# Attention followed by two expert layers: the sums of exponentials as matrix products with ones, four groups side by side, and GpSimd left with one kind of element-wise work

## The chip, the cores and the metric

The kernel runs on one core of one Trainium2 chip. The number that counts is the device time in microseconds (us) of one execution of the whole program; the runs of the kernel before have a median of 1322.9 us. Engine names in the rows: PE is TensorE (PEld its weight loads), DVE is VectorE, ACT is ScalarE, POOL is GpSimd, SP is SyncE, whose queue issues nearly all DMAs.

## The reference

Three stages, all in fp32. The change is in the first.

```
def _attn_ref(q, k, v, g_q, g_k):              # q, k, v: (4, 12, 448, 64)
    q_n, k_n = (rmsnorm(q, g_q), rmsnorm(k, g_k))
    scale = 1.0 / np.sqrt(q.shape[-1])
    scores = scale * np.matmul(q_n, k_n.transpose(0, 1, 3, 2))
    scores = scores - np.max(scores, axis=-1, keepdims=True)
    attn = np.exp(scores)
    attn = attn / (np.sum(attn, axis=-1, keepdims=True) + 1e-09)
    return np.matmul(attn, v).astype(np.float32)
...
    x = np.ascontiguousarray(attn_out.transpose(0, 2, 1, 3)).reshape(B * S, H * D)
    x = _moe_ref(x=x, **moe_kwargs)       # logits = x @ w_gate, 8 experts of 224 tokens, relu
    return _moe2_ref(x=x, **moe2_kwargs)  # h = x @ w_in; (h * cos(h)) @ w_out
```

## The kernel before

Two plans run one after the other. The first holds the attention, the router's logits, and, between them, the turning of 56 of 96 pieces of the last layer's 64-bit weights into pairs of 32-bit ones (tiles `nr` and `na`). The second holds the router, the experts, the last layer and the other 40 pieces.

**How work gets its place.** Every operation is first recorded as a `Step` with an engine, a cost in microseconds (`Plan.cost`) and what it reads and writes. `Plan.run` then places the steps in a simulated time and issues them in that order. `Plan.either` records one operation with two ways, VectorE and GpSimd; the planner takes the one that by its costs ends first. With `plan.shared` false, `either` means VectorE alone. On the chip each engine works through its instructions in the order that came out, and waits where an operand isn't there.

**The attention.** 48 heads are worked through as 24 pairs of two heads. For a pair, `front` loads queries and keys and gets the norms' roots (`squares`, `norm`); `turn` scales queries and keys by them (tile `qn`, by `either`), transposes them on TensorE (bank `t`) and splits them into a high and a low part (`hl` for queries, `kh` and `kl` for keys); SyncE's DMAs copy the parts into `tk` and `qs`. `shifts` gets upper bounds of the scores (seven products into bank `s`, seven maxima on VectorE into `cm`), and `copy` brings them as row `cr` into `qs`. `scores` multiplies (bank `st`, two of them), and ScalarE takes the exponential into a tile `pf`, 448 queries wide, with 112 keys in its partitions; four such tiles make one head. `weigh` multiplies the `pf` tiles with the values into bank `po`, the two heads of a pair side by side in 64 columns of the array each. `rows` gets the denominators and the router's logits, `tail` transposes and scales the output (`xk`), and `pair` stores it.

**What the change touches.** In `scores`, the four `pf` tiles of a head are added to one tile `sm` by three additions, on VectorE or GpSimd as the planner likes: 144 in all, of which the order has 130 on GpSimd and 14 on VectorE. In `rows`, once for three pairs, `ones` multiplies the `sm` tiles of the three pairs side by side, 32 columns of the array each, in two steps (head 0, head 1); a third step of the same shape multiplies the outputs `xe` with the router's weights `wg`. All three go into bank `dn`. One copy on ScalarE and four transposes then bring sums and logits to where VectorE takes the reciprocal. The last three pairs are done one at a time, with the three products side by side. `EASY` sends the low part of the queries from pair 2 on to GpSimd (ScalarE makes a second copy `f` for it, since GpSimd's operand has to lie in SBUF). `zset` fills constants before the first pair, `mix` (`mx`) gets two 64x64 corners of the queries for a pair's fourth bound, and in `Narrow.plan` a clamp of `na` and the last subtraction (`nr`) go to VectorE or GpSimd. The helper's line is L47, so rows are told apart by tiles.

Of the kernel before, what the change touches and what calls it, by code (L numbers as in the profile page):

```python
# [50 lines left out]
class Plan:  # L51
# [4 lines left out]
    def __init__(self, nc):  # L56
        self.nc, self.steps, self.seen, self.group, self.rush = nc, [], {}, None, 0.0
        self.shared, self.ahead = True, 0.0
# [217 lines left out]
UP = 3  # L276
# [3 lines left out]
NPF = 10  # L280
NSM = 9
# [6 lines left out]
EASY = 2  # L288
# [18 lines left out]
def attention(tc, P, R, ident, q, k, v, g_q, g_k, w_gate, x_dram, L, other):  # L307
# [4 lines left out]
    with ExitStack() as ctx:  # L312
# [32 lines left out]
        dns = ring("dn", 1, [96, S])  # L345
        xks = ring("xk", 2, [CP, NC, 2 * UP * D])
        recs = ring("r", 2, [CP, NC, 3, 2])
# [6 lines left out]
        def zset(t, val):  # L354
            P.either("memset", t.bitcast(F32), val)
# [48 lines left out]
        for _ in range(NSM):  # L404
            zset(sms()[96:CP + 1], 1.0)
        for t in mix:
            zset(t, 0.0)
        ve.tensor_scalar(gcol[:, 2:3], gcol[:, 0:1], gcol[:, 1:2], None, op0=ALU.mult)
# [19 lines left out]
        def turn(P_, i, rs, j):  # L428

            if True:  # L430
# [3 lines left out]
                mul = P.vector.tensor_tensor if P_ == 0 and i and QND else partial(P.either, "tensor_tensor")  # L434
# [123 lines left out]
        def weigh(P_):  # L558

            po = bo()[:, :S]  # L560
            t = vals.pop(P_).rearrange("p h (c d) -> p h c d", d=D)
            for c in range(NC):
                def both():
                    for h in range(2):
                        pe.matmul(po[h * D:(h + 1) * D], t[:, h, c], exps.pop((P_, h, c)), start=c == 0, stop=c == NC - 1)

                block(both)
            outs[P_] = xes()
            sc.activation(outs[P_], po, AF.Copy)

        def rows(ps):


            pd, dn, r, n = bd(), dns(), recs(), len(ps)
            steps = [[(ones[:, h], sums_of.pop((y, h))) for y in ps] for h in range(2)]
            steps.append([(wg[:, y % NP], outs[y]) for y in ps])
            if n == 1:
                steps = [[(ones[:, 0], x[0][1]) for x in steps[0:2]] + steps[2]]
            for k, row in enumerate(steps):
                def some():  # L580
                    for g, (w, x) in enumerate(row):
                        pe.matmul(pd[32 * g:32 * g + 32, :S], w, x, start=k == 0, stop=k == len(steps) - 1)

                block(some)
            sc.activation(dn, pd[0:96, :S], AF.Copy)
            p = bt()[0:CP, 0:NC * 96].rearrange("p (c g x) -> p c g x", c=NC, g=3)
# [787 lines left out]
```

## Time and profile before

| | us |
|---|---|
| median of three runs (1319.28 to 1332.39) | 1322.9 |
| the profiled execution | 1326.97 |
| its span from the first to the last instruction | 1325.1 |
| attention, by the engines' work | 0 to about 440 |
| router's first round, until the first expert's rows arrive | about 440 to 470 |
| experts and last layer | 470 to 1320 |

The profiled execution is 4 us above the median. The profile gives each engine's busy time in a stretch, the clock that TensorE was granted (1.00 is 2.4 GHz; the other level, 1.2 GHz, is 0.50), and, for the idle time before an instruction, who ended it. A matmul of fp32 operands leaves two records, a transpose and a product of reduced-precision operands (`F32R`) one.

### The profile page before, as it was taken

The page shows a single profiled execution, that of the slowest core. Times are in us where ns is not written, and L with a number is a line of the kernel's source. Part 1 is how long each engine was busy: PE and PEld are TensorE (multiplying, and loading weights), DVE is VectorE, ACT ScalarE, POOL GpSimd, SP SyncE. Part 2 cuts the span into 40 slices and gives each one's busy share as a digit, 9 for nine tenths or more (in the row PEclk, how much of TensorE's full clock was granted, in tenths as well). Part 3 has the DMA queues.
Part 4 walks back from the last instruction along what each step waited for, and adds up shares of the span by engine and source line. Part 5 has one row for each costly group of instructions (what it writes and reads, how often), then busy time and mean ns, then how long its engine had stood idle before and what let it go on. Part 6 is the DMA issues. An engine that isn't in the chain of part 4 may idle for free.

```text
span 1325.1 us, 20895 instructions
## 1 busy us (share of the span) xinstructions
PE 1194.0 (90%) x6807; PEld 954.3 (72%) x6807; DVE 978.0 (74%) x2641; ACT 671.5 (51%) x1657; POOL 317.7 (24%) x349
## 2 busy tenths in 40 slices
PE   6888887888988489999988999999999999899996
PEld 4444443433433289988877998889998889899996
DVE  8879999999898987989858658918657917655601
ACT  5566665655445354667345437625437615444500
POOL 4667676656755100000000200000200000100001
PEclk9789998878678678999988899999899999899998
DMA  8768787877755256988885767794677793676762
GB/s 198 169 166 206 205 210 201 233 191 199 202 164 161 95 152 202 287 306 278 302 258 188 208 202 231 231 296 120 190 210 228 245 282 109 167 214 220 239 218 74
DMA packets 207951, 273.53 MB, mean 206 GB/s; under 512 B 17473, under 2 KB 178530, under 8 KB 201698
## 3 DMA queue, kind: packets, MB, share of 16 engines
q1 hardware_dynamic: 205282, 261.18, 67.4%
q0 software_dynamic: 2560, 11.01, 2.8%
q8 instruction: 54, 0.88, 0.3%
q14 instruction: 55, 0.45, 0.1%
HBM read 202.79 MB, written 36.46 MB: 181 GB/s over the span
## 4 chain that ended last, share of the span: by engine, by line
PE 46%; DMA 11%; DVE 9%; issue 2%; ACT 1%; POOL 1%; SPq 0%; POOLq 0%; DVEq 0%; ACTq 0%
PE acc L47 42%; DMA wx<-w_out 2%; DMA xr<-x,idx 2%; DMA w_out<-nr 2%; PE tr L47 1%; PE rt L47 1%; DMA ws<-in_moe_w_dram 1%; DMA nr<-in_moe_w_out_dram 1%; DMA AB<-rows 1%; DVE wx L47 1%; DVE na L47 1%; DVE AB L47 1%; DVE oh L47 1%; DMA wx<-w_in 1%; DVE r L47 1%
## 5 line engine op out<-in xcount | busy, mean ns | idle before, releaser
L47 PE MATMUL acc<-gh,wx 128*128 128x224 f32 (+1 forms) x1952 | 376.9, 320 | 4.5 <-DMA wx<-w_out 3.0
L47 PEld LDWEIGHTS acc<-gh,wx 128*128 128x128 f32 x1952 | 290.8, 198 | 20.9 <-DMA wx<-w_out 6.5
L47 PE MATMUL acc<-x2h,wx 128*128 128x448 f32 x768 | 226.3, 372 | 0.0
L1155 POOL DMA_INDIRECT xr<-x,idx x16 | 18.0, 1125 | 640.5 <-issue 211.2
L47 PEld LDWEIGHTS acc<-x2h,wx 128*128 128x128 f32 x768 | 146.3, 190 | 16.5 <-issue 5.0
L47 DVE TENSOR_TENSOR wx<-ws,wx 128x768 fp32r<-128x768 f32 (+1 forms) x112 | 119.8, 1071 | 47.2 <-ACT wx L1194 43.1
L1194 ACT ACTIVATE wx<-ws 128x768 fp32r<-128x768 f32 (+1 forms) x104 | 98.1, 943 | 98.4 <-PE acc L47 82.7
L47 PE MATMUL acc<-gl,wx 128*128 128x448 f32 (+1 forms) x400 | 146.3, 366 | 0.0
L47 PE MATMUL acc<-xe,wx 128*128 128x224 f32 x1152 | 141.5, 284 | 0.3 <-DVE wx L47 0.2
L47 PE MATMUL acc<-x2l,wx 128*128 128x448 f32 x384 | 141.5, 369 | 0.0
L47 PEld LDWEIGHTS acc<-xe,wx 128*128 128x128 f32 x1152 | 138.2, 200 | 1.6 <-ACT wx L1194 0.8
L47 ACT ACTIVATE pf<-st 112x448 f32<-112x448 f32 x192 | 98.4, 541 | 67.5 <-PE st L47 63.5
L47 PE MATMUL st<-qs,tk 128*112 128x448 f32 (+1 forms) x384 | 124.4, 440 | 5.8 <-ACT pf L47 5.2
L47 DVE TENSOR_REDUCE cm<-s 128x1 f32<-128x448 f32 (+1 forms) x169 | 100.0, 615 | 29.6 <-PE s L47 29.3
L47 ACT ACTIVATE oh<-oh 128x896 bf16<-128x896 bf16 x80 | 75.3, 942 | 78.8 <-DVE oh L47 78.5
L47 PE MATMUL po<-pf,vr 112*64 112x448 f32 x384 | 108.6, 653 | 0.2 <-ACT pf L47 0.2
L47 POOL TENSOR_TENSOR sm<-sm,pf 112x448 f32<-112x448 f32 x87 | 103.4, 1205 | 16.3 <-ACT pf L47 9.4
L47 PEld LDWEIGHTS st<-qs,tk 128*112 128x112 f32 (+1 forms) x384 | 72.5, 208 | 47.9 <-ACT pf L47 17.0
L47 PE MATMUL s<-tk,qs 128*128 128x448 f32 (+2 forms) x146 | 64.5, 481 | 40.0 <-DVE cm L47 30.1
L47 DVE SCALAR_TENSOR_TENSOR na<-nr,na 128x256 int32<-128x256 int32 x192 | 97.9, 529 | 1.2
L47 ACT ACTIVATE r<-r 128x448 f32<-128x448 f32 x128 | 73.2, 574 | 32.4 <-DVE r L47 30.7
L47 DVE TENSOR_SCALAR oh<-AB,b 128x896 bf16<-128x896 f32 x80 | 51.2, 683 | 50.7 <-DMA AB<-rows 45.1
(248 smaller groups left out, 1919.0 us busy)
## 6 DMA issues: line engine op xcount, KB each, us to landing
wx<-w_in SPq DMA_DIRECT2D x64, 768.0 KB
wx<-w_out SPq DMA_DIRECT2D x48, 1024.0 KB
ws<-in_moe_w_dram SPq DMA_DIRECT2D x64, 384.0 KB
ws<-in_moe_w_dram SPq DMA_DIRECT2D x48, 512.0 KB
nr<-in_moe_w_in_dram SPq DMA_DIRECT2D x48, 256.0 KB
w_in<-nr SPq DMA_DIRECT2D x48, 256.0 KB
nr<-in_moe_w_out_dram SPq DMA_DIRECT2D x48, 256.0 KB
w_out<-nr SPq DMA_DIRECT2D x48, 256.0 KB
```

The costliest lines, as they stand in the source:

```text
L47: self.plan.add([(self.eng, self.plan.cost(self.eng, name, out, r, kw), lambda: f(*args, **kw))], r, w)
L1155: P.add([("POOL", 1.03, lambda x=x, h=h: nc.gpsimd.indirect_dma_start(out=x, out_offset=None, in_=x_rows, in_offset=bass.IndirectOffsetOnA ...
L1194: P.add([("ACT", 0.093 + n * 0.1067, lambda: nc.scalar.activation(hi, s, AF.Copy)), ("DVE", 0.07 + n * 0.0667, lambda: nc.vector.tensor_co ...
```

## The change

The additions go, and so do the tiles `sm`. In `weigh`, after the value products of a pair, `ones` multiplies the `pf` tiles themselves: the four tiles of a head at once, each in 32 columns of the array of its own, head 0 and then head 1, into the four 32-partition groups of bank `dn`. The 17 extra partitions that bring the 1e-9 move from `sm` to `pf`. `rows` works for one pair at a time: one product of 32 columns for the logits, added into the first group, a copy of 128 partitions, and, in place of four transposes, four fp32 products with `pick`, a 128x32 matrix that adds the four groups while it transposes. So reciprocal, copy and store come once a pair and not once in three. There are 18 `pf` tiles for 10.

`P.shared = False` is set once constants are filled, so that `either` means VectorE for the clamps and subtractions of `Narrow`, for `mix` and for the router's count. `EASY` and the copy `f` go: the low part of all queries is VectorE's. Constants are filled by GpSimd alone. The scaling of queries and keys is VectorE's in the first three pairs and GpSimd's in all others. The planner's costs for TensorE change too (`Plan.cost`), for both plans, so that the order changes all over.

```diff
-            return max(out.free_size() / 2400.0 + 0.0015, 0.105 if rhs.dtype == F32R else 0.0467) * passes
+            if name == "matmul" and rhs.dtype == F32 and self.beside:
+                passes *= {32: 0.32, 64: 0.6}.get(out.partition_size(), 1)
+            return max(out.free_size() / 2333.0 + 0.011, 0.107 if rhs.dtype == F32R else 0.0467) * passes
...
-        pfs = ring("pf", NPF, [CP, S])
-        pfs2 = ring("f2", 1, [128, S])
-        sms = ring("sm", NSM, [CP + 1, S])
+        pfs = ring("pf", NPF, [CP + 1, S])
...
-                mul = P.vector.tensor_tensor if P_ == 0 and i and QND else partial(P.either, "tensor_tensor")
+                mul = P.vector.tensor_tensor if P_ < UP else P.gpsimd.tensor_tensor
...
-                    if P_ >= EASY:
-                        f = pfs2()
-                        sc.activation(f, p[:, :S], AF.Copy)
-                        P.gpsimd.tensor_tensor(lo, f, hi.bitcast(F32), op=ALU.subtract)
-                    else:
-                        ve.tensor_tensor(lo, p[:, :S], hi.bitcast(F32), op=ALU.subtract)
+                    ve.tensor_tensor(lo, p[:, :S], hi.bitcast(F32), op=ALU.subtract)
...
-                    sc.activation(pf, p, AF.Exp)
-                    if c == 1:
-                        sums_of[P_, h] = sms()
-                    if c:
-                        s = sums_of[P_, h][0:CP]
-                        add = P.vector.tensor_tensor if P_ == NPR - 1 else partial(P.either, "tensor_tensor")
-                        add(s, exps[P_, h, 0] if c == 1 else s, pf, op=ALU.add)
+                    sc.activation(pf[0:CP], p, AF.Exp)
...
+            for h in range(2):
+                def four():
+                    for c in range(NC):
+                        n = CP + (c == 0)
+                        pe.matmul(pd[32 * c:32 * c + 32], ones[0:n, h], exps.pop((P_, h, c))[0:n], start=h == 0,
+                                  stop=h == 1 and c > 0)
+
+                block(four)
...
+            pd, dn, r = sums_of.pop(y), dns(), recs()
+            block(lambda: pe.matmul(pd[0:32], wg[:, y % NP], outs[y], start=False, stop=True))
+            sc.activation(dn, pd, AF.Copy)
+            p = bt()[0:CP, 0:NC * 32].rearrange("p (c x) -> p c x", c=NC)
             P.begin()
             for c in range(NC):
-                pe.transpose(p[:, c].rearrange("p g x -> p (g x)"), dn[:, c * CP:(c + 1) * CP], ident[0:96, 0:96])
+                pe.matmul(p[:, c, 0:18], dn[:, c * CP:(c + 1) * CP], pick[:, 0:18], start=True, stop=True)
...
+        P.shared = False
         AHEAD = 3
```

What the planner makes of it, on GpSimd first, in the middle of the attention. Before (`hl` is the low part of queries, `qn` their scaling, `sm` the sums, `na` a weight piece's clamp):

```order
L47 TENSOR_TENSOR hl_173<-f_200,hl_173 128x448
L47 TENSOR_TENSOR qn_171<-qk_158,rs_166 112x2x4x64
L47 TENSOR_TENSOR sm_208<-sm_208,pf_191 112x448
L47 TENSOR_TENSOR qn_172<-qk_158,rs_166 112x2x4x64
L261 TENSOR_SCALAR na_235<-na_235 128x256
L47 TENSOR_TENSOR sm_209<-pf_192,pf_194 112x448
L47 TENSOR_TENSOR sm_201<-pf_193,pf_195 112x448
L47 TENSOR_TENSOR sm_209<-sm_209,pf_196 112x448
L47 TENSOR_TENSOR sm_201<-sm_201,pf_197 112x448
```

Now, on GpSimd, from pair 3 on:

```order
L47 TENSOR_TENSOR qn_170<-qk_157,rs_166 112x2x4x64
L47 TENSOR_TENSOR qn_171<-qk_157,rs_166 112x2x4x64
L47 TENSOR_TENSOR qn_172<-qk_157,rs_166 112x2x4x64
L47 TENSOR_TENSOR qn_170<-qk_157,rs_166 112x2x4x64
L47 TENSOR_TENSOR qn_171<-qk_158,rs_166 112x2x4x64
L47 TENSOR_TENSOR qn_172<-qk_158,rs_166 112x2x4x64
```

In these stretches everything but the scaling is gone from GpSimd; of the 256 element-wise operations that the order had on GpSimd before (constants apart), 42 are left.

On TensorE, before, at a place where `rows` comes for three pairs (`po` value products, `st` scores, `s` bounds):

```order
L47 MATMUL po_228<-pf_196,vr_160 64x448
L47 MATMUL po_228<-pf_197,vr_160 64x448
L47 MATMUL s_224<-tk_144,qs_150 128x448
L47 MATMUL st_226<-qs_149,tk_141 112x448 x2
L47 MATMUL dn_229<-sm_201,ones 32x448
L47 MATMUL dn_229<-sm_203,ones 32x448
L47 MATMUL dn_229<-sm_205,ones 32x448
L47 MATMUL s_225<-tk_144,qs_150 128x448
L47 MATMUL dn_229<-sm_202,ones 32x448
L47 MATMUL dn_229<-sm_204,ones 32x448
L47 MATMUL dn_229<-sm_206,ones 32x448
L47 MATMUL dn_229<-xe_213,wg 32x448
```

Now, on TensorE, at the end of one pair (it is so in every pair):

```order
L47 MATMUL po_228<-pf_204,vr_161 64x448
L47 MATMUL po_228<-pf_205,vr_161 64x448
L47 MATMUL dn_229<-pf_198,ones 32x448
L47 MATMUL dn_229<-pf_200,ones 32x448
L47 MATMUL dn_229<-pf_202,ones 32x448
L47 MATMUL dn_229<-pf_204,ones 32x448
L47 MATMUL dn_229<-pf_199,ones 32x448
L47 MATMUL dn_229<-pf_201,ones 32x448
L47 MATMUL dn_229<-pf_203,ones 32x448
L47 MATMUL dn_229<-pf_205,ones 32x448
L47 MATMUL s_225<-tk_141,qs_149 128x448
L47 MATMUL t_222<-ident,xe_211 112x128 x4
```

The products with ones are 192 for 48, in 48 groups of four for groups of three, and they stand behind a pair's last value products; the one product with `wg` follows a few rows later, and the four with `pick` after that.

## Rows read from the trace of the kernel before

**Rows 1.** Busy time (instructions) of each engine by stage, TensorE's clock, DMA share, GB/s.

```profile
core 0: us, PE busy (x) PEld busy (x) DVE busy (x) ACT busy (x) POOL busy (x), PEclk, DMA share, GB/s
0.00:40.00 40.00, 27.15 (x175) 19.80 (x177) 33.28 (x125) 23.81 (x86) 21.93 (x56) 0.96 0.93 205
40.00:440.00 400.00, 336.00 (x1426) 165.15 (x1422) 361.84 (x770) 231.77 (x729) 260.13 (x244) 0.84 0.72 190
...
470.00:1320.00 850.00, 814.65 (x5125) 758.38 (x5123) 554.97 (x1569) 404.27 (x806) 33.32 (x46) 0.96 0.70 219
```

**Rows 2.** Waits in 40 to 440 us: total us, times, longest us.

```profile
PEld s L47 <- DVE cm L47: 51.0, 38, 5.6
PE s L47 <- DVE cm L47: 31.9, 14, 5.2
```

**Rows 3.** Groups on GpSimd, 40 to 440 us: count, busy us, mean ns, idle before.

```profile
L47 POOL TENSOR_TENSOR sm<-sm,pf 112x448 f32<-112x448 f32 x85 | 101.0, 1204 | 16.2 <-ACT pf L47 9.4 <-DVE sm L47 6.4
L47 POOL TENSOR_TENSOR sm<-pf,pf 112x448 f32<-112x448 f32 x42 | 50.6, 1218 | 10.1 <-ACT pf L47 10.1
L47 POOL TENSOR_TENSOR qn<-qk,rs 112x512 f32<-112x512 f32 x40 | 44.3, 1118 | 21.1 <-PE st L47 10.1 <-PE t L47 7.2 <-DVE rs L47 3.6
L47 POOL TENSOR_TENSOR nr<-na,nr 128x256 fp32r<-128x256 f32 x38 | 29.1, 770 | 62.9 <-ACT nr L47 57.7 <-DMA nr<-in_moe_w_in_dram 5.3
L47 POOL TENSOR_TENSOR hl<-f,hl 128x448 fp32r<-128x448 f32 x21 | 25.0, 1191 | 16.5 <-ACT f L47 16.4
```

**Rows 4.** Groups on VectorE, 40 to 440 us.

```profile
L47 DVE TENSOR_REDUCE cm<-s 128x1 f32<-128x448 f32 x161 | 95.2, 615 | 27.3 <-PE s L47 27.0
L47 DVE SCALAR_TENSOR_TENSOR na<-nr,na 128x256 int32<-128x256 int32 x110 | 63.4, 587 | 0.8
L47 DVE CAST mx<-hl 64x64 fp32r<-64x64 f32 x38 | 29.1, 766 | 2.1 <-ACT hl L47 1.8
L47 DVE TENSOR_SCALAR na<-na 128x256 int32<-128x256 int32 x55 | 26.6, 490 | 0.5 <-POOL na L261 0.2
...
L47 DVE TENSOR_SCALAR ab<-ia,X 112x128 bf16<-112x128 bf16 x16 | 10.2, 677 | 0.0
```

**Rows 5.** Groups on VectorE, 470 to 700 us, with GpSimd nearly idle.

```profile
L47 DVE SCALAR_TENSOR_TENSOR na<-nr,na 128x256 int32<-128x256 int32 x73 | 28.1, 419 | 0.3
...
L47 DVE TENSOR_SCALAR AB<-ia,X 112x128 bf16<-112x128 bf16 x80 | 15.5, 250 | 0.0
L47 DVE TENSOR_TENSOR nr<-na,nr 128x256 fp32r<-128x256 f32 x38 | 15.0, 418 | 1.1 <-ACT nr L47 1.1
...
L261 DVE TENSOR_SCALAR na<-na 128x256 f32<-128x256 f32 x37 | 10.3, 289 | 15.8 <-ACT na L47 15.5
...
L47 DVE TENSOR_TENSOR gl<-r,gh 128x448 fp32r<-128x448 f32 x16 | 9.8, 616 | 0.0
```

**Rows 6.** Tile mx, 40 to 440 us: shortest, median and longest in ns.

```profile
L47 DVE CAST mx<-hl x38: 177/826/2222, 40.3 to 398.2; 64x64 fp32r<-64x64 f32 x38
```

**Rows 7.** Two stretches of the attention, columns as in rows 1.

```profile
100.00:200.00 100.00, 83.71 (x400) 43.06 (x401) 97.56 (x203) 67.28 (x232) 70.87 (x64) 0.95 0.82 206
420.00:430.00 10.00, 9.13 (x44) 3.64 (x42) 9.24 (x15) 6.38 (x15) 6.84 (x6) 1.00 0.51 154
```

**Rows 8.** TensorE in order of time near 426 us: start, us, operation.

```profile
425.90 0.57 PE L47 MATMUL dn<-sm,ones 113*32 113x448 f32 x2
425.91 0.56 PE L47 MATMUL dn<-xe,wg 128*32 128x448 f32 x1
426.30 0.55 PE L47 MATMUL dn<-sm,ones 113*32 113x448 f32 x2
...
426.78 1.08 PE L47 MATMUL st<-qs,tk 128*112 128x448 f32 x4
...
430.18 0.54 PE L47 MATMUL t<-ident,dn 96*112 96x96 f32 x4
430.65 0.97 PE L47 MATMUL po<-pf,vr 112*64 112x448 f32 x4
```

More of the change, by code (lines that the diff above doesn't have):

```diff
@@ L57, in __init__ @@
         self.nc, self.steps, self.seen, self.group, self.rush = nc, [], {}, None, 0.0
-        self.shared, self.ahead = True, 0.0
+        self.shared, self.ahead, self.beside = True, 0.0, False
         self.tensor = Engine(self, "PE", nc.tensor)
@@ L279 @@
 TUNE_A = (3.5, 0.3, 4.5, 0.7, 30.0, 1.2)
-NPF = 10
-NSM = 9
+NPF = 18
 NXE = 6
@@ L287 @@
 HURRY_S = (0.0, 0.0)
-EASY = 2
 ACC = ()
@@ L340, in attention @@
         crs = ring("cr", 2, [2 * NC, 128], F32R)
-        pfs = ring("pf", NPF, [CP, S])
-        pfs2 = ring("f2", 1, [128, S])
-        sms = ring("sm", NSM, [CP + 1, S])
+        pfs = ring("pf", NPF, [CP + 1, S])
         xes = ring("xe", NXE, [128, S])
-        dns = ring("dn", 1, [96, S])
+        dns = ring("dn", 1, [128, S])
+        pick = cst.tile([128, 32], F32, name="pick")
         xks = ring("xk", 2, [CP, NC, 2 * UP * D])
-        recs = ring("r", 2, [CP, NC, 3, 2])
+        recs = ring("r", 3, [CP, NC, 2])
         abs_ = ring("ab", 1, [CP, 2, NC, 128], BF16)
@@ L354, in zset @@
         def zset(t, val):
-            P.either("memset", t.bitcast(F32), val)
+            P.gpsimd.memset(t.bitcast(F32), val)
         def load(src, P_, n, t):
@@ L403, in attention @@
             zset(ones[0:CP, j, j:j + 1], 1.0)
-        for _ in range(NSM):
-            zset(sms()[96:CP + 1], 1.0)
+        for _ in range(NPF):
+            zset(pfs()[96:CP + 1], 1.0)
         for t in mix:
             zset(t, 0.0)
+        ve.tensor_tensor(pick, ident[:, 0:32], ident[:, 32:64], op=ALU.add)
+        for j in range(2, 4):
+            ve.tensor_tensor(pick, pick, ident[:, 32 * j:32 * j + 32], op=ALU.add)
         ve.tensor_scalar(gcol[:, 2:3], gcol[:, 0:1], gcol[:, 1:2], None, op0=ALU.mult)
@@ L564, in both @@
                     for h in range(2):
-                        pe.matmul(po[h * D:(h + 1) * D], t[:, h, c], exps.pop((P_, h, c)), start=c == 0, stop=c == NC - 1)
+                        pe.matmul(po[h * D:(h + 1) * D], t[:, h, c], exps[P_, h, c][0:CP], start=c == 0, stop=c == NC - 1)
                 block(both)
+            sums_of[P_] = pd
+            P.beside = True
+            for h in range(2):
[5 more added lines that the diff above has]
+                block(four)
@@ L568, in weigh, with rows @@
+            P.beside = False
             outs[P_] = xes()
             sc.activation(outs[P_], po, AF.Copy)
[L571 to L586, printed above, removed]
+        def rows(y):
+            pd, dn, r = sums_of.pop(y), dns(), recs()
+            block(lambda: pe.matmul(pd[0:32], wg[:, y % NP], outs[y], start=False, stop=True))
+            sc.activation(dn, pd, AF.Copy)
+            p = bt()[0:CP, 0:NC * 32].rearrange("p (c x) -> p c x", c=NC)
@@ L587, in rows @@
             P.begin()
             for c in range(NC):
[L589 removed]
+                pe.matmul(p[:, c, 0:18], dn[:, c * CP:(c + 1) * CP], pick[:, 0:18], start=True, stop=True)
             P.finish()
[L591 to L599 removed]
+            ve.reciprocal(r, p[:, :, 0:2])
@@ L600, in rows @@
+            h = 2 * (y % NP)
+            ve.tensor_tensor(part[:, :, :, h:h + 2].rearrange("p c n h -> p c h n"),
+                             p[:, :, 2:18].rearrange("p c (h n) -> p c h n", h=2),
+                             r.unsqueeze(3).to_broadcast([CP, NC, 2, 8]), op=ALU.mult)
             return r
@@ L646, in finish @@
                 ve.tensor_reduce(part[:, :, :, H], part[:, :, :, 0:H - 2], AX.X, ALU.add)
-            if late or P_ % UP == UP - 1:
-                ps = [P_] if late else range(P_ - UP + 1, P_ + 1)
-                P.rush = END if P_ == NPR - 1 else 0.0
-                r = rows(ps)
-                todo.extend((y, r[:, :, j]) for j, y in enumerate(ps))
-                if P_ % NP == NP - 1:
-                    b = P_ // NP
-                    ve.tensor_reduce(L[:, b * NC:(b + 1) * NC, :], part[:, :, :, (H - 2) * late:H + late], AX.X, ALU.add)
-                    R.start(abs_(), b)
-                P.rush = 0.0
-            for _ in range(len(todo) if P_ >= NPR - LAST - 1 else 1):
-                if todo:
-                    pair(*todo.pop(0))
-        todo = []
+            P.rush = END if P_ == NPR - 1 else 0.0
+            r = rows(P_)
+            if P_ % NP == NP - 1:
+                b = P_ // NP
+                ve.tensor_reduce(L[:, b * NC:(b + 1) * NC, :], part[:, :, :, (H - 2) * late:H + late], AX.X, ALU.add)
+                R.start(abs_(), b)
+            P.rush = 0.0
+            pair(P_, r)
         def pair(P_, r):
```

12 lines of the change are left out of this document (2 added, 10 removed).

## The prediction

> **What bounds the kernel now.** I read the busy times by stage first, to find the stage that the change is in, then the waits in that stage, then the groups on VectorE and GpSimd there, and last TensorE's instructions in order of time for prices. The stages [rows 1] show a start of 40 us, 400 us of attention in its steady course, and 850 us of experts and last layer, with a short router round between. Only the attention's code changes. In its 400 us VectorE is busy for 362 us (90%) and TensorE for 336 us (84%) at a mean clock of 0.84; ScalarE with 232 us and the DMA engines with 0.72 have room. In the 850 us TensorE is busy for 815 us at 0.96. So the attention is held by VectorE, and TensorE, with less to do than it has time for, waits for it and falls to the lower clock. The waits say the same [rows 2]: TensorE's bounds `s` and their weight loads stood 32 and 51 us behind VectorE's maxima `cm`, which free the bank.
>
> VectorE itself is slowed. The maxima, which read a bank, take 615 ns each, as long as any pass over 448 elements [rows 4, 5]. But operations that read SBUF take much longer here than where GpSimd is idle: the `na` step with two tensors 587 ns against 419, a cast of 64 elements 766 ns with a shortest of 177, the `ab` comparison 677 against 250 [rows 4 to 6]. GpSimd is busy for 260 of the 400 us, in pieces of 0.8 to 1.2 us [rows 1, 3]. A VectorE operation that lasts one GpSimd operation too long fits that.
>
> **What the change takes from VectorE and gives to it.** GpSimd loses the sums (152 us), the `hl` and `nr` subtractions and the clamps, and keeps the scaling: 40 operations, 44 us [rows 3]. Its busy time in the stage falls from 260 to some 44 us, by 83%. I let VectorE's waiting for it fall by the same share. The waiting in four groups, by count and difference of means: `na` 110 x 168 ns = 18.5 us, shifts of `na` 55 x (490 - 289) = 11.1, `mx` 38 x (766 - 177) = 22.4, `ab` 16 x 427 = 6.8 [rows 4 to 6]; together 58.8 us, of which 83% is 49 us. The many smaller groups are not counted, so this is a lower bound of the relief; the upper one I don't price. VectorE gets 38 subtractions `nr` at 418 ns (15.9 us), 22 `hl`, 448 wide, for which the row of the same width and two tensors is `gl`, 616 ns (13.6), 11 clamps at 289 ns (3.2) and 8 corners `mx` at 177 ns (1.4); it loses 14 additions at no less than 616 ns (8.6) [rows 5, 6]. Sum: 362 - 49 + 25.5 = 338 us at most. At the 90% of now that is 374 us of stage instead of 400.
>
> **What it gives to TensorE.** Prices at full clock come from 420 to 430 us, where 1.00 was granted [rows 7]. There one step of three products side by side starts at 425.90, its second records at 426.30, and the next work at 426.78: 0.88 us, and 0.80 is twice the distance of the records, without the change of shape before and after [rows 8]. Before, there are 24 such steps (seven groups of three pairs with three each, three pairs with one): 21.1 us; and ten times four transposes of `dn` at 0.47 us [rows 8], 4.7 us. Now there are 48 groups of four. No row shows four; the two records of a step of three start 0.01 us apart, so I take 0.88 for four as well: 42.2 us. The bounds are 0.80, and 0.88 x 4/3 = 1.17 if a fourth product costs its share. The 24 single products with `wg` are put at 0.88 too, 21.1 us (lower bound 0.80). The four products with `pick` stand in for four transposes, in fp32 and so with two records for one: 0.94 us a pair, 22.6 us, lower bound 0.47. Added: 42.2 + 21.1 + 22.6 - 25.8 = +60 us, between +43 and +74.
>
> On packing in columns the trace and the Trainium skill differ. Three products side by side took 0.88 us where three alone would take at least 3 x 0.80, a gain of 2.7 [rows 8]. The Trainium skill ("TensorE: Matmul & The Clock Gate", section "Measured speedup vs the span model") gives 2.38 for three column tiles and 3.07 for four tiles in rows, so less than the row shows. By 3.07 a group of four would take 4 x 0.80 / 3.07 = 1.04 us, TensorE would have 8 us more, and the predicted time would be some 8 us higher. I keep the row's.
>
> **Which of the two ends last.** TensorE's present work in the stage, at full clock, is 336 x 0.84 = 282 us of 400 [rows 1]; with the addition 342 us (325 to 356). It becomes the engine with most to do. What an engine in that place reaches, waits and clock included, the later stage shows: 815 x 0.96 = 782 us in 850, a share of 0.92 [rows 1]. 342 / 0.92 = 372 us, close to the 374 that VectorE's bound gave. So I expect the stage to take 372 us for 400: 28 us less.
>
> **Covers and other parts.** ScalarE loses 22 copies `f` and gets 14 more of `dn`: nothing, at 232 of 400 us; without that room it would be a gain too. The sums no longer wait for additions, but bank `dn` is single: a pair's first group of four must wait until the pair before has been copied out, a chain of value products, copy, `wg` and copy, some 3 us by an estimate of four steps of 0.6 to 0.9 us, as rows of 448 columns are [rows 5, 8], in a pair's 15 us; I cost it at nothing, and at the rest of that chain, 1 to 2 us a pair, if the value products slip late. The exponentials' 18 tiles hold the four of a head until its sums are made. In the first 40 us VectorE loses ten memsets and takes six scalings, while GpSimd fills 18 strips in place of 8; the first scaling waits there for the norm, not for constants: nothing, bounds -2 and +3 us. The planner's new TensorE costs shuffle the second plan too; its instructions stay, so I take nothing, with 6 us either way, a sixth of the 35 us that TensorE idles there [rows 1]. DMAs are the same; 0.72 of 400 us is 288 us, and 77% of 372.
>
> **The sum** is made against the profiled execution: span 1325.1 us, 1.9 us outside it. 1325.1 - 28 = 1297 us of span, 1299 for the execution. That execution was 4 us above the median, so against the median it is 1322.9 - 28 = 1295 us, 2.1% less.
>
> **Rivals.** *More than that:* without VectorE's hold TensorE runs nearly dense and at full clock, as in 420 to 430 us [rows 7], and the added work is at its lower end: 325 / 0.95 = 342 us, 58 us less, 1265. For it: all small SBUF operations of VectorE are relieved too. Against it: not even the last layer reaches 0.95. *No change:* TensorE reaches a share of 0.86 only, because a pair's `st`, exponential and `s` go back and forth in small steps through two banks each: 342 / 0.86 = 398 us, 1321. *Slower:* TensorE's added products are a cost on the engine that now ends last, and its share stays at what the best 100 us of the attention show, 83.71 x 0.95 = 79.5 of 100 [rows 7]: 342 / 0.795 = 430 us, 30 us more, 1353. The place is a pair's end, where value products and eight sums stand in a row and ScalarE and VectorE run dry, so that TensorE waits and falls in clock right after. It decides from a share below 342/400 = 0.855. Against it: in those 100 us VectorE was 98% busy, and that hold is loosened. *The change doesn't do what it says:* the four groups follow one another, 4 x 0.80 us each, 111 us more for TensorE, (342 + 111) / 0.92 = 492 us, 1415. Three do run side by side [rows 8], so hardly.
>
> **How the numbers follow.** My forecast, 1295 with 1276 to 1312 for the added work between +43 and +74, has a chance of 0.42; more than that 0.20; no change 0.18; slower 0.17; not side by side 0.03. The range of 8 in 10 goes from 1263, the dense case with 2 us of the start, to 1336, half way from no change to the slower case. This kernel's measurements can tell about 1% (13 us) from no change. Faster by more is the forecast but for a little above 1310, and the dense case: 0.61; within 1% the rest of the forecast and no change: 0.20; slower 0.19.
>
> **What would show it.** Right: in the profile after, the attention ends some 28 us earlier; `na` with two tensors near 420 ns and `mx` near 180; GpSimd near 50 us in the stage; waits of `s` for `cm` down by more than half; TensorE's clock there above 0.92; groups of four about 0.9 us apart. Wrong: if `na` stays near 590 ns the reading of VectorE's slowness fails; if TensorE's clock stays near 0.84 with many waits, its share was set too high; if the sums take over 60 us at full clock, their price was; and if 470 us onward moves by more than 6 us, the second plan's new order decides.

## The result, and the profile after

The changed kernel takes **1278.8 us** (median of four runs, 1276.6 to 1281.1), the kernel before 1325.5 us (four runs beside it, 1319.3 to 1332.4): a ratio of 0.9646 with an interval from 0.9592 to 0.9700, so 3.5% faster. The forecast was 1295 us, 2.1% less: right in sign and place, too small in size.

The profiled execution of the changed kernel took 1281.1 us, its span 1279.0 us. Its page shows GpSimd nearly empty, and a first third in which TensorE's clock is no longer down; columns are the busy time, its share of the span and the count of instructions, and then the clock in 40 slices.

```profile
PE 1191.9 (93%) x7247; PEld 955.5 (75%) x7247; DVE 889.9 (70%) x2710; ACT 673.6 (53%) x1655; POOL 99.9 (8%) x156
...
PEclk9999998999995899999989999999999999999998
```

Where the time went is read from two marks that both traces have: the first product of the router's last round (`rt<-tot`), which is the end of the attention, and the first transposes of an expert's rows (`tr`). From the order of time on TensorE (start, us, operation, idle time before), first of the kernel before, then of the changed one:

```profile
441.13 0.34 PE L47 MATMUL rt<-tot,up 128*128 128x2 f32 x1 [0.74 <-DVE t L47]
469.70 1.01 PE L47 MATMUL tr<-ident,xr 112*128 112x112 f32 x4 [0.91 <-DMA xr<-x,idx]
```

```profile
389.24 0.34 PE L47 MATMUL rt<-tot,up 128*128 128x2 f32 x1 [0.87 <-DVE t L47]
418.04 0.95 PE L47 MATMUL tr<-ident,xr 112*128 112x112 f32 x4
```

The attention ends 51.9 us earlier, the experts start 51.7 us earlier, and the span is 46.1 us shorter: everything was gained in the attention, and 5.6 us were given back behind it (what they are comes below, with the planner's costs). The windows of the changed kernel, cut to its stages, stand against [rows 1] in the same columns:

```profile
0.00:40.00 40.00, 29.48 (x176) 21.07 (x177) 27.38 (x105) 23.49 (x81) 16.37 (x64) 0.95 0.96 219
40.00:388.00 348.00, 331.98 (x1865) 174.14 (x1863) 281.74 (x864) 228.45 (x726) 46.21 (x42) 0.97 0.81 216
418.00:1268.00 850.00, 814.10 (x5122) 748.89 (x5121) 550.88 (x1559) 409.91 (x813) 30.91 (x38) 0.97 0.70 218
```

VectorE, which was busy for 90% of its stage, is busy for 81% of a shorter one: 282 us instead of 362, although it has more operations. TensorE went from 84% at a clock of 0.84 to 95% at 0.97; its work at full clock is 332 x 0.97 = 322 us in 348, a share of 0.925.

The groups on VectorE in that stretch (count, busy us, mean ns) say why it has less to do. Against [rows 4], `cm`, which reads a bank, is what it was; the four SBUF groups of [rows 4] that are shown here are shorter, and close to the rows of a stretch with an idle GpSimd where [rows 5] has them. Not everything from SBUF is shorter: the reduction `ss` takes 676 ns and took 677 before, the first row here.

```profile
L47 DVE TENSOR_REDUCE ss<-sq 112x8 f32<-112x512 f32 x18 | 12.1, 677 | 0.9 <-ACT sq L47 0.8
```

```profile
L47 DVE TENSOR_REDUCE cm<-s 128x1 f32<-128x448 f32 x161 | 95.4, 616 | 33.4 <-PE s L47 32.6
L47 DVE SCALAR_TENSOR_TENSOR na<-nr,na 128x256 int32<-128x256 int32 x112 | 45.9, 436 | 0.3
...
L47 DVE TENSOR_SCALAR na<-na 128x256 int32<-128x256 int32 x55 | 15.8, 303 | 0.1
...
L47 DVE TENSOR_REDUCE ss<-sq 112x8 f32<-112x512 f32 x18 | 12.2, 676 | 0.1
L47 DVE CAST mx<-hl 64x64 fp32r<-64x64 f32 x42 | 11.1, 263 | 0.3
...
L47 DVE TENSOR_SCALAR ab<-ia,X 112x128 bf16<-112x128 bf16 x16 | 3.3, 244 | 0.0
```

The waits turned round. TensorE's bounds `s` stood 32 us, and their weight loads 51 us, behind VectorE's maxima before [rows 2]; now it is 2.5 and 7.6 us. VectorE waits for TensorE's `s` for 33 us, 27 before [rows 4] (us in all, times, longest):

```profile
DVE cm L47 <- PE s L47: 32.6, 33, 2.2
...
PEld s L47 <- DVE cm L47: 7.6, 9, 2.1
...
PE s L47 <- DVE cm L47: 2.5, 2, 1.9
```

The new products in order of time on TensorE, at a granted clock of 1.00:

```profile
183.29 2.48 PE L47 MATMUL po<-pf,vr 112*64 112x448 f32 x12
185.69 1.71 PE L47 MATMUL dn<-pf,ones 113*32 113x448 f32 x16
187.33 0.48 PE L47 MATMUL s<-tk,qs 128*128 128x448 f32 x1
...
188.38 0.94 PE L47 MATMUL dn<-xe,wg 128*32 128x448 f32 x2
189.25 1.08 PE L47 MATMUL st<-qs,tk 128*112 128x448 f32 x4
...
192.19 0.97 PE L47 MATMUL po<-pf,vr 112*64 112x448 f32 x4
193.09 0.96 PE L47 MATMUL t<-pick,dn 128*112 128x18 f32 x8
193.90 0.66 PE L47 MATMUL s<-tk,qs 128*128 128x448 f32 x2
```

From start to the next start, two groups of four take 1.64 us, 0.82 each; a single product with `wg` takes 0.87, and the four with `pick` 0.81. Three steps of `po` in a row take 2.40, one alone 0.90.

### The profile page after: what moved, and what is told of

Read it like the earlier page. It is cut to its first block, busy times and chain, and to the rows that moved or that the text cites. A ratio compares the mean times of both kernels' runs of the same rounds, so it can differ in the third digit from the quotient of the medians.

```text
span 1279.0 us, 21567 instructions
## 1 busy us (share of the span) xinstructions
PE 1191.9 (93%) x7247; PEld 955.5 (75%) x7247; DVE 889.9 (70%) x2710; ACT 673.6 (53%) x1655; POOL 99.9 (8%) x156
## 4 chain that ended last, share of the span: by engine, by line
PE 60%; DMA 16%; DVE 16%; ACT 2%; SPq 2%; issue 2%; POOL 0%; POOLq 0%; DVEq 0%; ACTq 0%
PE acc L47 37%; PE st L47 5%; PE po L47 5%; PE dn L47 4%; PE t L47 3%; PE s L47 3%; DMA AB<-rows 3%; DVE r L47 2%; DMA w_out<-nr 2%; DMA nr<-in_moe_w_out_dram 2%; DVE oh L47 2%; DMA wx<-w_out 2%; DVE AB L47 2%; DVE na L47 1%; PE rt L47 1%
## 5 line engine op out<-in xcount | busy, mean ns | idle before, releaser
L47 PEld LDWEIGHTS acc<-gh,wx 128*128 128x128 f32 x1952 | 285.3, 194 | 27.7 <-issue 8.8
L47 PE MATMUL acc<-x2h,wx 128*128 128x448 f32 x768 | 229.9, 375 | 0.0
L1179 ACT ACTIVATE wx<-ws 128x768 fp32r<-128x768 f32 (+1 forms) x110 | 103.0, 937 | 101.7 <-PE acc L47 71.0
L47 PE MATMUL acc<-xe,wx 128*128 128x224 f32 x1152 | 138.0, 281 | 1.0 <-DVE xe L47 0.7
L47 PE MATMUL st<-qs,tk 128*112 128x448 f32 (+1 forms) x384 | 107.4, 391 | 5.1 <-ACT pf L47 3.1
L47 PE MATMUL po<-pf,vr 112*64 112x448 f32 x384 | 88.6, 566 | 0.0
L47 PEld LDWEIGHTS st<-qs,tk 128*112 128x112 f32 (+1 forms) x384 | 62.8, 180 | 31.0 <-ACT pf L47 11.0
L47 PEld LDWEIGHTS acc<-gl,wx 128*128 128x128 f32 x400 | 77.7, 194 | 6.7 <-DVE gl L47 1.4
L47 PEld LDWEIGHTS acc<-x2l,wx 128*128 128x128 f32 x384 | 73.6, 192 | 5.7
L47 DVE SCALAR_TENSOR_TENSOR na<-nr,na 128x256 int32<-128x256 int32 x192 | 76.4, 428 | 0.5
L1140 POOL DMA_INDIRECT xr<-x,idx x16 | 16.9, 1058 | 689.7 <-issue 212.9
```

The source lines that it names most:

```text
L47: self.plan.add([(self.eng, self.plan.cost(self.eng, name, out, r, kw), lambda: f(*args, **kw))], r, w)
L1140: P.add([("POOL", 1.03, lambda x=x, h=h: nc.gpsimd.indirect_dma_start(out=x, out_offset=None, in_=x_rows, in_offset=bass.IndirectOffsetOnA ...
L1179: P.add([("ACT", 0.093 + n * 0.1067, lambda: nc.scalar.activation(hi, s, AF.Copy)), ("DVE", 0.07 + n * 0.0667, lambda: nc.vector.tensor_co ...
```

## The experiments

Two theories stood at the start. **A:** the gain comes from VectorE, which GpSimd's work no longer slows, and TensorE ends last in the attention now. **B:** it comes from the rest of the change (the order that the planner's new costs give, the shorter chain to the denominators, the element-wise work that leaves a late GpSimd queue), and the pace is set by the banks that go from engine to engine. All ratios are to the kernel before, run beside the experiment (medians of 1328.0, 1323.0 and 1325.0 us, in three sets).

### Work on GpSimd that nobody needs

The changed kernel with, behind every exponential,

```
+ P.gpsimd.tensor_copy(gate[0:1, 0:1], pf[0:1, 0:1])
+ P.gpsimd.tensor_tensor(sink, gate, gate, op=ALU.add)
```

> The changed kernel with idle work put back on GpSimd: after every exponential a copy of one element and an addition of 448 elements that reads SBUF and whose result nobody uses, 192 of each. The result of the program is the same. Theory (GpSimd operations that read SBUF make VectorE's operations on SBUF wait, and VectorE then holds TensorE): GpSimd busy some 270 us in the attention, the na step with two tensors from 436 back towards 590 ns, mx from 263 towards 770, the attention's end 25 to 50 us later, 1305 to 1330 us. Rival A (GpSimd's own lateness held the kernel before, its sums coming too late for what waited on them): nobody waits for the idle work, so 1279 us, within 8. Rival B (the gain comes from the planner's new costs and its order): also 1279, within 8.

It took 1321.9 us (1319.0 to 1329.6), ratio 0.9961 (0.9929 to 0.9994): the gain was gone, as theory A had it. The second kernel replaced the addition by three fills:

```
+ for _ in range(3):
+     P.gpsimd.memset(gate, 0.0)
```

> The same with three fills of 448 elements, which read nothing, in place of each idle addition; GpSimd about as long busy. Theory, if it is reading that blocks: na with two tensors stays below 470 ns and the time within 10 us of 1279. If any GpSimd operation blocks VectorE: as with the reads, 1305 to 1330. Rivals A and B: 1279, within 8.

It took 1345.6 us, ratio 1.0142 (1.0056 to 1.0228), slower than before; that expectation missed. Its window (columns as in [rows 1]) shows what had been overlooked: VectorE has 312 us to do in 400, but GpSimd, at 346 us, is full, and the scaling `qn` that TensorE needs stands in its queue; TensorE's transposes `t` and their weight loads waited 9.9 us for GpSimd here.

```profile
40.00:440.00 400.00, 361.02 (x1826) 167.74 (x1825) 311.99 (x848) 225.23 (x716) 345.90 (x758) 0.97 0.72 189
```

So both kernels mixed slower operations on VectorE and a scaling that comes late. They mixed in a third thing: by their traces TensorE, VectorE and ScalarE work through another order than in the changed kernel. The first two were parted, at one order, with a changed kernel in which VectorE scales all pairs, and nobody waits for GpSimd:

```
- mul = P.vector.tensor_tensor if P_ < UP else P.gpsimd.tensor_tensor
+ mul = P.vector.tensor_tensor
```

> The changed kernel with the scaling of queries and keys on VectorE for every pair, so that GpSimd has nothing to do in the attention. VectorE gets 42 products of 512 elements, some 0.6 us each as its other passes of two tensors (hl 614 ns): 26 us more, 309 of the 348 us from 40 to 388. Theory (TensorE ends last there, VectorE has room): the same time as the changed kernel, 1275 to 1285 us. Rival (VectorE still sets the pace at its 0.81 of the stage): 309/0.81 = 381 us for 348, so 1312 us.

1282.4 us (1277.6 to 1286.0), ratio 0.9677 (0.9608 to 0.9745): as theory A expected. To this kernel came the idle additions again; the traces show the order on the other engines unchanged:

> The kernel with all scaling on VectorE, to which GpSimd gets behind every exponential a copy of one element and an addition of 448 elements from SBUF whose result nobody reads; nobody waits for GpSimd here, and the order on the other engines is the same. It parts the two things that idle work on GpSimd did at once when the scaling stood in its queue. Theory (work that reads SBUF on GpSimd stretches VectorE's operations): na with two tensors goes from about 440 to 600 ns or more, mx from under 250 to over 400, VectorE's busy time rises by 60 us, and the attention ends 30 us or more later than with an idle GpSimd: 1310 us or more. Rival (what cost time before was only that the scaling came late out of GpSimd's queue): within 5 us of the kernel with all scaling on VectorE.

1309.6 us (1305.2 to 1322.1), ratio 0.9921 (0.9885 to 0.9958): 27 us over the kernel without them, run beside it. That is just under the 1310 expected, and `na` went to 500 ns only, not 600. And with two fills in place of the addition:

> The kernel with all scaling on VectorE, to which GpSimd gets behind every exponential a copy of one element and two fills of 448 elements, which only write, in place of the addition that reads; nobody waits for GpSimd, and the order on the other engines is the same. Theory (fills stretch only VectorE's operations on one tensor, and what they cost is VectorE's time alone; the lateness of the kernel with fills in the scaling's queue was the queue's): na with two tensors stays under 450 ns, na with one goes from 287 to over 400, mx from 185 to over 300, and the time is 8 to 20 us over the kernel with idle GpSimd, 1290 to 1302 us. Rival one (fills cost nothing once nobody waits for GpSimd): 1277 to 1287 us. Rival two (any work on GpSimd costs alike, reading or writing): as with additions, 1305 us or more.

1290.1 us (1286.7 to 1293.3), ratio 0.9733 (0.9693 to 0.9772): 8 us more than with GpSimd idle, at the low end of what was expected, while the one-tensor `na` took 361 ns and not the expected 400. The intervals of the two ratios overlap, and in the traces the attention ends at 400.4 us with GpSimd idle and at 400.0 us with fills; so that fills cost the kernel time isn't shown. The windows of the three kernels to the end of the attention (columns as in [rows 1]), first with GpSimd idle, then with additions, then with fills:

```profile
40.00:400.00 360.00, 342.30 (x1884) 179.04 (x1882) 292.10 (x915) 233.53 (x736) 0.00 (x0) 0.96 0.78 212
```

```profile
40.00:420.00 380.00, 348.36 (x1865) 178.81 (x1864) 353.23 (x908) 232.66 (x726) 247.84 (x377) 0.94 0.74 199
```

```profile
40.00:400.00 360.00, 338.82 (x1867) 176.87 (x1867) 307.52 (x912) 231.13 (x726) 231.43 (x567) 0.96 0.78 212
```

And their groups on VectorE from 40 to 370 us, in the same order:

```profile
L47 DVE TENSOR_REDUCE cm<-s 128x1 f32<-128x448 f32 x154 | 90.7, 618 | 32.3 <-PE s L47 31.2
L47 DVE SCALAR_TENSOR_TENSOR na<-nr,na 128x256 int32<-128x256 int32 x96 | 36.5, 417 | 0.1
...
L47 DVE TENSOR_REDUCE ss<-sq 112x8 f32<-112x512 f32 x18 | 12.1, 679 | 0.5 <-ACT sq L47 0.5
L47 DVE TENSOR_SCALAR na<-na 128x256 int32<-128x256 int32 x47 | 12.0, 287 | 0.1
L47 DVE CAST mx<-hl 64x64 fp32r<-64x64 f32 x43 | 8.0, 185 | 0.3
```

```profile
L47 DVE TENSOR_REDUCE cm<-s 128x1 f32<-128x448 f32 x150 | 87.9, 613 | 12.1 <-PE s L47 11.4
L47 DVE SCALAR_TENSOR_TENSOR na<-nr,na 128x256 int32<-128x256 int32 x88 | 41.0, 500 | 0.1
...
L47 DVE CAST mx<-hl 64x64 fp32r<-64x64 f32 x38 | 16.3, 429 | 0.3
...
L47 DVE TENSOR_SCALAR na<-na 128x256 int32<-128x256 int32 x43 | 13.1, 333 | 0.1
...
L47 DVE TENSOR_REDUCE ss<-sq 112x8 f32<-112x512 f32 x18 | 12.1, 674 | 0.7 <-ACT sq L47 0.7
```

```profile
L47 DVE TENSOR_REDUCE cm<-s 128x1 f32<-128x448 f32 x155 | 91.1, 616 | 27.5 <-PE s L47 27.0
L47 DVE SCALAR_TENSOR_TENSOR na<-nr,na 128x256 int32<-128x256 int32 x96 | 36.3, 414 | 0.1
...
L47 DVE TENSOR_SCALAR na<-na 128x256 int32<-128x256 int32 x47 | 15.6, 361 | 0.1
L47 DVE CAST mx<-hl 64x64 fp32r<-64x64 f32 x42 | 15.0, 356 | 0.3
...
L47 DVE TENSOR_REDUCE ss<-sq 112x8 f32<-112x512 f32 x18 | 12.1, 677 | 0.4 <-ACT sq L47 0.4
```

Additions stretch three of these groups: two tensors 417 to 500 ns, one tensor 287 to 333, the cast 185 to 429. Fills leave two tensors alone (417 and 414 ns) and stretch one tensor (287 to 361) and the cast (185 to 356). The maxima `cm`, which read a bank, take 613 to 618 ns in all three, and the reduction `ss`, which reads SBUF, 674 to 679. That GpSimd's work slows VectorE is shown, and for the additions that this moves the end. Little else can have moved it: in that trace ScalarE waited 4.5 us for GpSimd, whose one-element copy reads its tile, and TensorE's weight loads 1.4 us; with fills it was 3.6 and 2.1 us. The Trainium skill ("SBUF — State Buffer", section "Who interferes with whom") has this rule: an operation of VectorE with two SBUF inputs contends with work on GpSimd that reads SBUF and not with work that only writes, copies, casts and operations of a tensor with scalars contend where they use two ports, and reductions never do. The three traces agree in the groups shown; which of them use two ports no trace shows.

### TensorE's work at an unchanged order

A first attempt left out the group of four for the odd heads and let the even heads' sums stand in:

```
- for h in range(2):
+ for h in range(1):
```

> The changed kernel without the second head's group of four in each pair; head 0's sums then divide both heads, so the output differs. TensorE loses 24 groups, 21 us at full clock. If TensorE ends last in the attention, as forecast: 21/0.92 = 23 us less, 1256, and 1250 to 1262. If VectorE or ScalarE holds the attention now: less than 8 us, 1271 to 1279.

1284.5 us, ratio 0.9681 (0.9598 to 0.9765): with some 20 us less for TensorE it wasn't faster at all. But the planner had written out another order for it, on TensorE, VectorE and ScalarE alike, so it told nothing about work alone. The next two keep the order on every engine, as their traces show, by giving the edit no cost, or the old one, in the planner. One adds a group of four with zero weights (a third row of `ones`, left at zero) to each pair, the other cuts the second group to 112 columns:

```
+ for c in range(NC) if h else ():
+     P.add([("PE", 0.0, lambda ...: nc.tensor.matmul(pd[32 * c:32 * c + 32], ones[0:CP, 2], x[0:CP], start=False, stop=False))], ...)
```

> The changed kernel with a second group of four products a pair, of the same sizes, whose weights are zeros, so that the output stays the same; the order on every engine is the same. 24 groups at 0.82 us are 19.7 us of TensorE at full clock. Theory (TensorE ends last in the attention, at a share of 0.925): 19.7/0.925 = 21 us more, 1300 us. Rival (the hand-over of banks between TensorE, ScalarE and VectorE sets the pace, and TensorE has its 16 us of idle time and 3% of clock to give): at most 8 us more, 1279 to 1287 us.

```
+ x, m = exps.pop((P_, h, c))[0:n], CP if h else S
+ cost = P.cost("PE", "matmul", pd[32 * c:32 * c + 32], [ones, x], {})
+ P.add([("PE", cost, lambda ...: nc.tensor.matmul(pd[32 * c:32 * c + 32, 0:m], ones[0:n, h], x[:, 0:m], ...
```

> The changed kernel with the second group of four of each pair cut from 448 to 112 columns, the order on every engine being the same; left out are three quarters of the sums of the odd heads, for which the even heads' sums stand in. 24 groups lose three quarters of 0.82 us, 14.8 us of TensorE at full clock. Theory (TensorE ends last): 14.8/0.925 = 16 us less, 1263 us. Rival (banks handed over set the pace): the same time, 1275 to 1283 us.

More work: 1289.3 us (1280.5 to 1290.7), ratio 0.9722 (0.9646 to 0.9798). Less: 1272.4 us (1267.5 to 1281.3), ratio 0.9600 (0.9529 to 0.9671). Neither theory's number came. The windows from 40 us to the end of the attention, more work first, columns as in [rows 1], each with the mark of that end:

```profile
40.00:399.00 359.00, 346.12 (x2055) 179.21 (x2051) 280.64 (x864) 228.84 (x726) 46.24 (x42) 0.98 0.78 211
```

```profile
399.80 0.34 PE L47 MATMUL rt<-tot,up 128*128 128x2 f32 x1 [0.87 <-DVE t L47]
```

```profile
40.00:391.00 351.00, 330.83 (x1868) 180.23 (x1866) 281.67 (x862) 227.81 (x726) 45.32 (x42) 0.94 0.81 216
```

```profile
392.50 0.34 PE L47 MATMUL rt<-tot,up 128*128 128x2 f32 x1 [0.87 <-DVE t L47]
```

TensorE's work at full clock is 346 x 0.98 = 339 us in the one and 331 x 0.94 = 311 us in the other; between their medians lie 16.9 us. So a microsecond of TensorE's work counts for 17/28 = 0.6 us, or 0.5 by the 34.5 us put in and left out; the intervals of the two ratios overlap at their edges, so this is no sharper than "about half". By the ends of the attention in the two traces, 399.8 and 392.5 us, it would be 7.3/28 = 0.3, but the trace with less work is of an execution of 1281.3 us, 9 over that kernel's median. The rest is taken from idle time, which goes from 20 to 13 us, and from the clock, which is 0.94 in the one trace and 0.98 in the other.

### Undoing one part

The additions back on GpSimd (144 of them), with one product with ones a head, two of 0.8 us a pair, in place of the two groups of four:

```
+ P.gpsimd.tensor_tensor(s, exps[P_, h, 0] if c == 1 else s, pf, op=ALU.add)
+ pe.matmul(pd[0:32], ones[:, h], adds.pop((P_, h)), start=h == 0, stop=False)
```

> The changed kernel with the exponentials' additions back on GpSimd, all 144 of them, and one product with ones a head (two of some 0.8 us a pair, as long as the two groups of four), with 11 exponential tiles and 9 sum tiles; the rest of the change stays. TensorE has the same work, GpSimd some 150 us more. Theory (reading work on GpSimd is what costs, 31 us for 230 us of it in the kernel with idle additions): 196 us of GpSimd against 46 cost 20 us, and the scaling that stands behind additions some more: 1298 to 1312 us. Rival (the gain came from the rest of the change, clamps, subtractions, corners and the single rows of the denominators): 1275 to 1288 us.

1347.3 us (1344.3 to 1355.8), ratio 1.0195 (1.0141 to 1.0249): slower than before, and 35 us over the top of what was expected. Its window, and two of its groups on VectorE (40 to 370 us):

```profile
40.00:453.00 413.00, 366.25 (x1587) 184.85 (x1585) 359.24 (x869) 230.40 (x728) 211.64 (x183) 0.91 0.68 184
```

```profile
L47 DVE SCALAR_TENSOR_TENSOR na<-nr,na 128x256 int32<-128x256 int32 x74 | 40.4, 572 | 0.1
...
L47 DVE CAST mx<-hl 64x64 fp32r<-64x64 f32 x36 | 19.7, 546 | 0.3
```

VectorE is back at 359 us, with the operations that the change gave it and the slowness of before. The kernel also has 11 exponential tiles for 18, and an order of its own, so not all of the 68 us over the changed kernel need be the additions'.

The narrowing's `nr`, 29 clamps and the corners `mx` free to go to GpSimd again, by leaving out one line:

```
- P.shared = False
```

> The changed kernel with the narrowing's subtraction nr, 29 clamps and the corners mx free to go to GpSimd again: it takes 56 nr, 29 clamps and 46 corners beside the scaling, by the rows of before some 75 us more, and VectorE loses some 45 us of its own. Theory (GpSimd's work costs more than it relieves): 75 us of reading and copying work cost 10 us by 31 for 230, VectorE's 45 us less bring 45 x 3.7/26 = 6 us by the kernel with all scaling on VectorE: 1280 to 1290 us. Rival (VectorE is relieved, and that decides): 1265 to 1275 us.

1270.8 us (1268.4 to 1273.4), ratio 0.9590 (0.9549 to 0.9631): the expectation missed and its rival was right. The interval overlaps that of the changed kernel (0.9592 to 0.9700), so that it is better is likely and not shown. GpSimd has 132 us here instead of 46, and VectorE 264 us instead of 282:

```profile
40.00:383.00 343.00, 331.19 (x1870) 177.66 (x1867) 264.02 (x741) 228.59 (x726) 132.44 (x165) 0.97 0.84 221
```

```profile
L47 DVE SCALAR_TENSOR_TENSOR na<-nr,na 128x256 int32<-128x256 int32 x105 | 44.3, 440 | 0.7
L47 DVE TENSOR_SCALAR na<-na 128x256 int32<-128x256 int32 x51 | 19.0, 383 | 0.7 <-POOL na L263 0.5
```

Two tensors take 440 ns, as in the changed kernel (436), one tensor 383 for 303. So this work on GpSimd takes more from VectorE than it costs it. The order is another one too, so the time can't be put down to that alone.

### The planner's costs

The kernel before with the new TensorE costs alone, and the changed kernel with the old ones in its second plan:

```
+ if name == "matmul" and rhs.dtype == F32:
+     passes *= {32: 0.32, 64: 0.6}.get(out.partition_size(), 1)
+ return max(out.free_size() / 2333.0 + 0.011, 0.107 if rhs.dtype == F32R else 0.0467) * passes
```

> The kernel before with the planner's new TensorE costs alone, which change the order and none of the instructions; products with 32 and 64 columns count for 0.32 and 0.6 of before. Theory (the gain comes from what GpSimd no longer does, and not from the order): 1315 to 1330 us, as before. Rival (part of the gain is the new order's): 1300 us or less.

```
+ second.old = True
```

> The changed kernel, but the second plan (router, experts, last layer) gets the old TensorE costs, so that its order is that of before. If the new order costs the 5.6 us by which the later stages are longer than before, they shrink from 861 to 855 us and the whole takes 1273 us. If those 5.6 us are spread between executions: 1279, within 3.

The first took 1337.3 us, ratio 1.0088 (1.0057 to 1.0119): a little slower than before, and 7 us over the expected range, so the order that these costs give to the same work isn't where the gain is from. The second took 1278.3 us, ratio 0.9633 (0.9570 to 0.9696), as the changed kernel; so the old order doesn't bring the 5.6 us given back behind the attention. They lie within what executions differ by: from the mark `rt<-tot` to the end the traces of all fourteen kernels show 883 to 894 us, and the two with additions and with fills on GpSimd, whose order is the same throughout, 883.0 and 891.5 us.

## Why the prediction was right, and where its sizes were not

**What did not hold.** The forecast rests on TensorE ending last in the attention, at the last layer's share of 0.92. Its added work came nearly as written, and the result lies within the forecast's bounds, but TensorE alone doesn't set the end. That 322/0.92 = 350 us is so near the measured 348 is in part luck, as the next paragraphs show.

**Neither engine ends last.** Five kernels have TensorE's work within 321 to 329 us (busy time by clock) and let no result wait behind idle work on GpSimd. Put in the order of VectorE's busy time from 40 us to the end of the attention, read from the same windows, their medians are (the medians of the kernel before, beside them, lie within 0.4%):

| kernel | VectorE, us | median, us |
|---|---|---|
| `nr`, clamps, corners shared | 264 | 1270.8 |
| changed kernel | 282 | 1278.8 |
| all scaling on VectorE | 292 | 1282.4 |
| the same, with fills on GpSimd | 308 | 1290.1 |
| the same, with additions on GpSimd | 353 | 1309.6 |

From end to end that is 38.8 us for 89 us, 0.44 us per microsecond of VectorE, and the three between lie within 1 us of that line, closer than runs of one kernel agree. The last three rows have one order throughout: from 292 to 353 us the median grows by 27.2 us, 0.45, and the end of the attention in the traces, 400.4 and 420.5 us, by 0.33. TensorE's work counts for 0.3 to 0.6. So, as far as these runs tell, the pace of the attention is set by both in turn: TensorE makes `s`, VectorE takes its maximum, and TensorE makes the next in the bank that comes free; what either saves the other gives back in part.

**The terms.** VectorE's relief was put at 49 us or more, in four groups. They gave 110 x (587 - 436) = 16.6 us for `na` with two tensors, 55 x (490 - 303) = 10.3 for its shifts, 38 x (766 - 263) = 19.1 for `mx` and 16 x (677 - 244) = 6.9 for `ab`, 53 us in all: right as a lower bound. But VectorE's whole was put at 338 us at most, and it is 282: the smaller groups, not counted, gave the rest of the fall from 362 us, which with the 25.5 us that VectorE was to get is some 105 us. The reading of [rows 4 to 6], that GpSimd stretches VectorE's operations on SBUF, held, and the kernels with additions and fills show it.

TensorE's added work was mis-sized a little: 48 x 0.82 + 24 x 0.87 + 24 x 0.81 - 25.8 = 54 us, not 60. The groups of four run side by side as forecast (0.82 us, against 0.88 taken), and the products with `pick` were 3 us cheaper. The gain for four tiles in rows that the Trainium skill states ("TensorE: Matmul & The Clock Gate", section "Measured speedup vs the span model") would have made a group 1.04 us; the measurement decides against it here. TensorE's whole work came out at 322 us, not 342; the other 14 us lie in the products that both kernels have. One part shows in the rows: a step of `po` takes 0.80 in a row of three and 0.90 alone, and the rows are longer now. Another part is how 282 was made, a mean busy time by a mean clock: summed over stretches of 10 us it is 280 us before and 324 us after, and in the first 40 us 26 and 28 us. And busy time by clock is no fixed amount of work: the changed kernel's products, without one more, come to 336 us with the idle additions and to 356 us with the fills of the first two experiments. How the rest divides is open.

**The step that was too small** is the stage, 342/0.92 = 372 us, where 348 were measured. The kernel with a group added has the work that was forecast, 339 us, and its attention ends at 399.8, after 360 us: so at the work that was forecast the stage is still 12 us shorter than forecast, mostly by the share, which was 0.945 there and not 0.92. For the changed kernel itself the share fits, 0.925, and the term that was mis-sized is TensorE's work: 20 us at 0.92 are 22 of the 24 us. The share was carried over from another stage as a constant; in the three traces it is 0.886, 0.925 and 0.945 at 311, 322 and 339 us, the first from that execution 9 us over the median. The forecast's upper end, 1312, is 1310 by its own sum; nothing hangs on it.

**Where the gain is from.** By the two slopes, VectorE's 80 us less are worth 80 x 0.44 = 35 us, and TensorE's 40 us more cost 20. That leaves 47 - 35 + 20 = 32 us for which VectorE's and TensorE's amounts don't account, an estimate from these rows; with slopes of 0.33 to 0.44 and 0.3 to 0.6 it is 24 to 45 us. The kernel with the additions back lies as far off the line: 359 us of VectorE would give 1312 us, and it took 1347, 35 more. What both have, and the five on the line don't, is additions on GpSimd whose sums others need, and 10 or 11 exponential tiles for 18; the kernel with fills ahead of the scaling is off the line too, 1345.6 us with VectorE busy for 312 us of 400. That the 32 us are waits for results from a slow queue would fit, but the traces speak against it: all waits of the other engines for GpSimd in the attention come to 11 us before, to 1 us in the changed kernel, and to 3 us with the additions back, where GpSimd itself waits 132 us for exponentials. The fewer tiles and the order remain, and no run parts them. So what these 32 us are is open; that the whole change brings 47 us is measured.

**The small terms.** Start, ScalarE and the single bank `dn` at nothing: in the first 40 us TensorE was busy for 29.5 us, with 27.2 before; ScalarE has 228 of 348 us; TensorE's waits for the copies around that bank come to 2.2 us in the stage. The second plan at nothing, with 6 us either way: 5.6 us, within what executions differ by.

**The rivals.** "Slower" rested on a share of 0.795 with VectorE at 98%; the trace after shows 0.925, with VectorE at 81%. "More than that", 1265, was 14 us from what came and the forecast 16 us; it wanted a share of 0.95 at 325 us, where 0.925 at 322 us came, and the last layer's 0.92, held against it, isn't a limit: 0.945 was reached with 339 us. "No change" took a hand-over in small steps, which fits these runs, but at a price that they don't show, a share of 0.86 at 342 us. "Not side by side" falls with 0.82 us for a group.

## What to carry to other kernels

Where two engines hand small pieces to each other, don't look for the one that ends last: price each engine's work by what a microsecond of it moves the end, which one kernel with idle work added and one with work cut, at an unchanged order, can tell, if the effect is clear of what executions differ by. Before work goes to GpSimd, count what it does to VectorE's other operations on SBUF; idle additions for 248 us here added 61 us to VectorE's 292 us, while a subtraction, clamps and corners took more from VectorE than they cost it. An experiment that adds work or leaves it out must keep the order, or it measures the planner.

## What the runs showed of the hardware that was not expected

Fills on GpSimd lengthen some of VectorE's operations: two of 448 elements behind each exponential took the cast of 64 elements from 185 to 356 ns and the shift of 256 from 287 to 361, with the pass over two tensors at 414 ns; the attention's end stayed at 400 us in the traces. Four fp32 products with 32 columns each run side by side at nearly the time of one, 0.82 us for a group, while a single product, standing between others, took 0.87. And at the same order of instructions TensorE's granted clock in the stage was 0.94, 0.97 and 0.98 at 311, 322 and 339 us of work, in one trace each, the first 9 us over its kernel's median; that the clock goes up with the work is a reading of three traces and not shown.
